# First pair of an attention and SwiGLU kernel: from both batches together to one batch after the other, with another fixed order of the parts

## The chip, the cores and the metric

The kernel runs on one core of one Trainium2 chip. The metric is the device time of one execution in microseconds (us); a time of the kernel is the median over several runs. The core has TensorE (PE in the profile; PEld is its weight load), VectorE (DVE), ScalarE (ACT), GpSimd (POOL) and SyncE (SP), which issues the DMAs. Work buffers are in SBUF; TensorE writes to PSUM, which is divided into banks.

## What is computed

Attention with 32 memories a head, for 8 batches, 8 heads, 576 positions and 64 values a head, and behind it a normalised SwiGLU block on 4608 tokens of 512 values:

```python
a = exp(phi - max(phi)); a = a / (sum(a) + 1e-09)
k_m = einsum('bhsm,bhsd->bhmd', a, k)
v_m = einsum('bhsm,bhsd->bhmd', a, v)
scores = (q @ k_m.T) / sqrt(64)
attn = softmax(scores)
x = (attn @ v_m), heads side by side
xn = x / sqrt(mean(x * x) + 1e-06) * rms_g
g = xn @ w_gate; val = xn @ w_val
out = (silu(g) * val) @ w_out
```

`w_gate` and `w_val` are 512 x 1536, `w_out` is 1536 x 512. All arrays are float32.

## The kernel before, in words

The eight batches are worked in four pairs, `pr` 0 to 3. The product `attn @ v_m` is never sent through the gate as `x`: `v_m` (with `rms_g` in it, `vm`) is multiplied with the weights first (`vw_steps`: `vp`, split into a high part `xh` and a low part `xl`), and the gate products `pg` and `pv` (`gv_steps`, L1069) then take the attention `at`, scaled by the token's root `rinv` and split into `ath` and `atl`, as their other operand. `x` itself is made once (`xp`, L845), for the sum of its squares alone. Behind the gate stand `sg` (silu, ScalarE), `hf` (product, VectorE), its parts `hh` and `hl`, and the output product `po` (L1126), summed in `acc` and stored. Products of high and low parts stand in for one float32 product.

Pair 0 has a path of its own, and it is what the change is about. For each batch `b` the k and v of a half (`load_half`, L331) and `phi` are loaded, `prep` makes the exponentials `e_bd`, and `kv_steps(b)` makes `kvp` (products of k or v with `e_bd`, L461, and with `ones`, L471), then on VectorE `si`, `im`, `kb` and `vb` (L480 to L496), on TensorE the transpose `kvt` (L511), and on ScalarE `km` (L519); `vt` becomes `vm` on GpSimd (L533). Then come the scores, by head pair `s` of four and by group of tiles (the 9 tiles of a batch are in `GROUPS` of 4 and of 5). One array holds both batches: `load_q` (L546) puts the q of batch `j` on every second partition, `q_steps` copies it in order (`qr`, L553), transposes it (`qtp`, L567) and copies it back (`qT`, L573). `score_steps` multiplies it with the `km` of both batches (`S`, L589), and VectorE makes the maximum `mxs` (L599), the difference `ex` (L603) and, behind the exponential of ScalarE (L608), the sum `sm` (L612 to L618). GpSimd divides, and the result stands in `first` (L624).

`x_steps(0)` then takes `first` by two tiles: transposes `tp` (L747), copies into `at` (L757), `xp` and its squares with their sums `ssq` (L856), the root chain `fin` in two groups of tiles (12 VectorE rows each, L866 to L891, result `rinv`), and for every tile a diagonal matrix of its `rinv` on ScalarE (`diag`, L803), with which TensorE multiplies `first`, so that transposing and scaling are one product (`ts`, L811). ScalarE copies the high part of `ts` out (`ath`, L830), VectorE subtracts it for the low part (`atl`, L826).

The pairs 1 to 3 go through `attend_steps` and the other branch of `x_steps`. Beside all this, the weights are loaded as `raw`, scaled by powers of two and split (`convert`: `wex`, L948 and L960 on VectorE, `wc` and `w` on GpSimd, L981).

What sets the order: every step above is appended to a list, `parts`, in the order of the program; `perform` then runs the parts in the order of the table `ISSUE`, and each engine's queue, SP's DMA queue too, takes its instructions in that order. No scheduler comes behind it. PSUM tiles of one bank are handed out by `bank`, from four buffers that rotate under one tag (L271); SBUF buffers are handed out by tags in the order in which the parts ask for them.

## Time and profile before

| | |
|---|---|
| median of three runs | 793.31 us (793.02 to 795.59) |
| the profiled execution | 792.07 us |
| its span, first to last instruction | 790.3 us |
| mean granted TensorE clock | 0.991 |
| PE busy | 748.9 us (95%) |
| PEld busy | 639.0 us (81%) |
| DVE busy | 471.8 us (60%) |
| ACT busy | 350.9 us (44%) |
| POOL busy | 244.4 us (31%) |
| DMA | 112.86 MB, 143 GB/s in the mean |

Busy times are of the profiled execution and are shares of its span. PE and PEld overlap. A row of the time line is one instruction or a few alike, with its start, its length, the engine, the line, the operation, what it writes and reads, and in brackets the idle time of the engine ahead of it and what ended that. A row of the waits says which engine waited for which, in how many pieces and for how long. In the stretches, the granted clock is a share of 2.4 GHz.

### The profile page before, as it was taken

How to read it: one execution, taken by the hardware profiler on the slowest of the kernel's cores; microseconds unless marked ns; L12 is line 12 of the kernel's file. 1: busy time of each engine (PE TensorE's matmuls, PEld its weight loads, DVE VectorE, ACT ScalarE, POOL GpSimd, SP SyncE). 2: the span in 40 equal slices, each digit the busy share in tenths (PEclk: the TensorE clock that was granted, in tenths of full speed). 3: DMA queues.
4: the chain of work that ended last, by engine and by line, in shares of the span. 5: the costliest groups of instructions: out<-in, count | busy, mean ns of one | idle time of the engine just before them, and what ended most of it. 6: DMA issues, size and time to landing. Idle time of an engine off the chain costs nothing.

```text
span 790.3 us, 18128 instructions
## 1 busy us (share of the span) xinstructions
PE 748.9 (95%) x7496; PEld 639.0 (81%) x7496; DVE 471.8 (60%) x956; ACT 350.9 (44%) x697; POOL 244.4 (31%) x209
## 2 busy tenths in 40 slices
PE   4777988999999999999999999899999999999998
PEld 2565766788887988888888888788888888888886
DVE  6698878888776676465565374655454422444443
ACT  1668767665555544532354334442432335232221
POOL 0244555354432223322433212221232212121212
PEclk9799999999999999999999999999999999999999
DMA  9947775856583652253153654222241334112113
GB/s 331 375 148 214 200 184 198 275 177 213 196 216 85 198 152 95 80 174 98 67 181 123 153 170 99 86 81 71 92 134 54 117 110 147 53 56 80 54 54 120
DMA packets 111722, 112.86 MB, mean 143 GB/s; under 512 B 61460, under 2 KB 77848, under 8 KB 111640
## 3 DMA queue, kind: packets, MB, share of 16 engines
q1 hardware_dynamic: 111640, 111.70, 45.2%
q8 instruction: 59, 0.97, 0.5%
q14 instruction: 23, 0.19, 0.1%
HBM read 89.66 MB, written 22.02 MB: 141 GB/s over the span
## 4 chain that ended last, share of the span: by engine, by line
PE 81%; DVE 6%; ACT 5%; DMA 4%; SPq 2%; issue 1%; POOL 0%; ACTq 0%; DVEq 0%
PE po L1126 36%; PE pg L1069 17%; PE pv L1069 17%; PE vp L1034 5%; PE xp L845 2%; SPq L645 2%; DMA kvs<-in_k_dram 1%; PE kvp L461 1%; DMA qs<-in_q_dram 1%; PE S L670 1%; ACT wex L944 1%; DVE phi L407 1%; ACT xh L1051 1%; DMA raw<-in_moe_w_out_dram 1%; ACT L1080 1%
## 5 line engine op out<-in xcount | busy, mean ns | idle before, releaser
L1100 POOL TENSOR_TENSOR hl<-hf,hh 128x512 fp32r<-128x512 f32 (+1 forms) x84 | 120.0, 1431 | 311.8 <-ACT hh L1095 297.9
L1085 DVE TENSOR_TENSOR hf<-pv,sg 128x256 f32<-128x256 f32 (+1 forms) x192 | 85.5, 452 | 153.1 <-PE pv L1069 110.1
L1126 PE MATMUL po<-oh,hh 128*128 128x512 f32 x432 | 172.2, 399 | 2.3 <-ACT acc L1135 1.4
L1080 ACT ACTIVATE sg<-pg 128x256 f32<-128x256 f32 (+1 forms) x192 | 77.6, 411 | 213.9 <-PE pg L1069 183.3
L1137 DVE TENSOR_TENSOR acc<-po,acc 128x512 f32<-128x512 f32 x180 | 121.0, 685 | 84.5 <-PE po L1126 84.0
L1126 PE MATMUL po<-oh,hl 128*128 128x512 f32 x432 | 170.2, 394 | 0.0
L1126 PE MATMUL po<-ol,hh 128*128 128x512 f32 x432 | 169.2, 392 | 0.0
L1095 ACT CAST hh<-hf 128x512 fp32r<-128x512 f32 (+1 forms) x96 | 64.5, 675 | 86.5 <-DVE hf L1085 86.2
L1126 PEld LDWEIGHTS po<-oh,hh 128*128 128x128 f32 x432 | 81.1, 188 | 21.8 <-ACT acc L1135 2.2
L1126 PEld LDWEIGHTS po<-oh,hl 128*128 128x128 f32 x432 | 81.2, 188 | 17.9
L1126 PEld LDWEIGHTS po<-ol,hh 128*128 128x128 f32 x432 | 81.2, 188 | 13.5
L1069 PE MATMUL pv<-ath,xh 128*128 128x320 f32 (+1 forms) x384 | 84.6, 301 | 4.3 <-ACT sg L1080 3.3
L1069 PE MATMUL pg<-ath,xh 128*128 128x256 f32 (+1 forms) x384 | 85.8, 305 | 2.4 <-DVE hf L1085 1.4
L1069 PE MATMUL pv<-ath,xl 128*128 128x320 f32 (+1 forms) x384 | 81.4, 293 | 0.0
L1069 PE MATMUL pg<-ath,xl 128*128 128x256 f32 (+1 forms) x384 | 81.3, 293 | 0.0
L1069 PE MATMUL pg<-atl,xh 128*128 128x256 f32 (+1 forms) x384 | 81.3, 293 | 0.0
L1069 PE MATMUL pv<-atl,xh 128*128 128x320 f32 (+1 forms) x384 | 81.3, 293 | 0.0
L1049 DVE TENSOR_TENSOR xl<-vp,xh 128x512 fp32r<-128x512 f32 x96 | 64.3, 682 | 28.0 <-ACT xh L1051 27.8
L1069 PEld LDWEIGHTS pg<-ath,xh 128*128 128x128 f32 x384 | 62.7, 188 | 16.7 <-issue 5.0
L1069 PEld LDWEIGHTS pv<-ath,xh 128*128 128x128 f32 x384 | 63.4, 188 | 15.3 <-ACT sg L1080 5.3
L1051 ACT CAST xh<-vp 128x512 fp32r<-128x512 f32 x96 | 54.3, 590 | 29.8 <-PE pv L1069 11.7
L1069 PEld LDWEIGHTS pv<-atl,xh 128*128 128x128 f32 x384 | 61.3, 188 | 0.0
(121 smaller groups left out, 998.0 us busy)
## 6 DMA issues: line engine op xcount, KB each, us to landing
wc<-wd SPq DMA_DIRECT2D x36, 512.0 KB, 5.5
oh<-od SPq DMA_DIRECT2D x36, 256.0 KB, 3.6
ol<-od SPq DMA_DIRECT2D x36, 256.0 KB, 3.9
out_dram<-acc SPq DMA_DIRECT2D x36, 256.0 KB, 2.2
q<-in_q_dram SPq DMA_DIRECT2D x96, 72.0 KB, 2.9
raw<-in_moe_w_val_dram SPq DMA_DIRECT2D x12, 512.0 KB, 4.7
raw<-in_moe_w_gate_dram SPq DMA_DIRECT2D x12, 512.0 KB, 4.5
raw<-in_moe_w_out_dram SPq DMA_DIRECT2D x12, 512.0 KB, 4.7
```

Source lines behind the costliest of these rows:

```text
L645: load(d["q", cc][32 * g:32 * g + 32, s], q[b, 4 * cc + 2 * s + h].rearrange("(r x) d -> r x d", r=32)[:, :, 32 * half:32 * half + 32],)
L845: nc.tensor.matmul(xp[64 * j:64 * j + 64, s, t - t0, P * cc:P * cc + P], st["at", pr][rows, t, cc, 64 * j:64 * j + 64], st["kb", 2 * pr + ...
L1034: nc.tensor.matmul(vp[32 * g:32 * g + 32, flip(b, cc), cc, :], vm[pr][rows, b, hp, 32 * (g % 2):32 * (g % 2) + 32], w[rows, hp, :], start= ...
L1049: V.tensor_tensor(out=xl[:, k], in0=src, in1=xh[:, k].bitcast(F32), op=ALU.subtract)
L1051: nc.scalar.copy(xs[i][0][:, k], src)
L1069: nc.tensor.matmul(pt[:, :N], l[:, flip(b, cc), cc, half * P:half * P + P], r[:, b, cc, t0:t0 + n, :].rearrange("p t x -> p (t x)"), start ...
L1080: nc.scalar.activation(sg[:, :N], acts[gi, b, 0][:, :N], AF.Silu)
L1085: V.tensor_tensor(out=acts[gi][:, :, b, :], in0=acts[gi, b, 1][:, :N].rearrange("p (t x) -> p t x", x=64), in1=acts[gi, b, 2][:, :N].rearr ...
L1095: nc.scalar.copy(hh, acts[gi].rearrange("p t b x -> p t (b x)"))
L1100: (V if gi and i < 12 else nc.gpsimd).tensor_tensor(out=hl, in0=acts[gi].rearrange("p t b x -> p t (b x)"), in1=hsplit[i, gi][0].bitcast(F ...
L1126: nc.tensor.matmul(po, l[:, tt, :], r, start=(m == 0), stop=(m == 5))
L1137: V.tensor_tensor(out=accs[key], in0=pt[0], in1=accs[key], op=ALU.add)
```

## The change

Pair 0 is worked batch by batch. `load_q(j, s, half)` loads the q of one batch and two heads onto 64 partitions, so that one tile of scores holds four heads of one batch; each batch has two `s` in place of the four for both. In the list, `q_steps`, `score_steps` and the new `first_steps` of batch 0 stand before batch 1's. `first_steps(j)` takes the place of the pair 0 branch of `x_steps`. It transposes `first` (`tp`) by pieces of 4, 4 and 1 tiles, copies them (the middle piece on VectorE), and packs two tiles into one `xp` of 128 partitions, so that five squares a batch are left. As a token's sum then stands on either half of the partitions, a small product with a constant `twice` (which GpSimd makes at the start) puts them in order (`ss`, two products a batch). One root chain a batch follows, 12 VectorE rows of 9 columns. `scaled` then multiplies `first` by the root on GpSimd (three pieces a batch), TensorE transposes the result (`ts`), and `put` makes the high and low parts, three and three a batch.

Also: `bank` takes the bank of each tile from a table `BANKS`, one digit a call, from four tags of one buffer each; 17 SBUF tags get their place by small tiles ahead of everything else; and the table `ISSUE` is new in full.

The diff, cut:

```diff
-ON_SCALAR = 21
+
+BANKS = (
+    "012301230123012312132031203120310231032103213203012101231231200232332320312310230302031203103213"
...
+)
 
 ISSUE = [
-    31, 0, 37, 12, 38, 39, 13, 1, 40, 19, 14, 15, 20, 42, 2, 3, 21, 16, 17, 4, 5, 34, 22, 23, 24, 36, 18, 6,
...
+    24, 2, 25, 26, 27, 28, 17, 18, 29, 50, 30, 19, 20, 21, 22, 8, 36, 23, 31, 1, 32, 33, 37, 38, 0, 39, 40,
...
+    tiny = persist.tile([P, 64], F32, name="tiny")
...
+    BANK = "".join(BANKS)
+    turn = [0]
+
     def bank(name, shape=None):
-        return ps.tile(shape or [P, 512], F32, tag="b", name=name, bufs=4)
+        turn[0] += 1
+        return ps.tile(shape or [P, 512], F32, tag="b" + BANK[turn[0] - 1], name=name, bufs=1)
...
+    for tag, n in (
+        ("acc0", 1), ("acc1", 1), ("hf0", 1), ("mc", 4), ("mxp", 2), ("sg", 2), ("xh", 2), ("si", 2), ("im", 2),
+        ("hh0", 3), ("hl1", 3), ("hl0", 3), ("hh1", 3), ("xl", 2), ("mxs", 2), ("sm", 2), ("hf1", 1),
+    ):
+        sb.tile([P, 1], F32, tag=tag, name=f"{tag}_first", bufs=n)
...
-    def load_q(s, j):
-        load(st["q", s][j::2], q[j, 2 * s:2 * s + 2].rearrange("h (p c) d -> p h (c d)", c=NT))
+    def load_q(j, s, half):
+        hp = 2 * half + s
+        load(
+            st["q", j][64 * half:64 * half + 64, s],
+            q[j, 2 * hp:2 * hp + 2].rearrange("h (p c) d -> p h (c d)", c=NT),
+        )
+
+    def twice():
+        st["twice"] = tw = sb.tile([P, 2, 2, 64], F32, tag="hl0", name="twice", bufs=3)
+        nc.gpsimd.memset(tw, 0.0)
...
+    def first_steps(j):
...
+        def both():
+            d["ss"] = tp = bank(f"ss{j}")
+            for i in range(2):
+                nc.tensor.matmul(
+                    tp[:, i:10 - i:2], st["twice"][:, i].rearrange("p a x -> p (a x)"), st["ssq"][:, j, :5 - i],
+                    start=True, stop=True,
+                )
...
+        def scaled(t0, n):
+            def f():
+                nc.gpsimd.tensor_tensor(
+                    out=st["first"][:, 1, j, t0:t0 + n], in0=st["first"][:, 0, j, t0:t0 + n],
+                    in1=r[:, t0:t0 + n].unsqueeze(2).broadcast_to([P, n, P]), op=ALU.mult,
+                )
+            return f
...
+        steps = []
+        for t0, n in PIECES:
+            steps += [turn(t0, n, 0), copy(t0, n)]
+        for u0 in range(0, 5, 2):
+            steps += [mm(u0)] + [square(x) for x in range(u0, min(u0 + 2, 5))]
+        steps += [both, root]
+        for t0, n in PIECES:
+            steps += [scaled(t0, n), turn(t0, n, 1), put(t0, n, 0), put(t0, n, 1)]
+        return steps
...
-            def diag(t):
-                def f():
-                    d["dg", t] = dg = st["first"][:, NT * 256 + t * P:NT * 256 + (t + 1) * P]
-                    nc.scalar.activation(dg, ident, AF.Copy, scale=rinv[pr][:, t:t + 1])
-                return f
...
-        if pr == 0:
-            return steps + [scaled(t0) for t0 in range(0, NT, 2)]
...
-    load_phi(1)
-    for cc in range(2):
-        for i in range(2):
-            load_half(0, cc, i)
-    add(prep(0, 0, 2), prep(0, 2, 4)[:-1], prep(1))
-    add(load_rg, put_rg)
-    first_q = [[lambda s=s, j=j: load_q(s, j) for j in range(2)] for s in range(HP)]
-    add(first_q[:2])
+    add([lambda cc=cc, i=i: load_half(0, cc, i) for cc in range(2) for i in range(2)])
+    add([lambda s=s, half=half: load_q(0, s, half) for s in range(2) for half in range(2)])
+    add(lambda: load_phi(1))
     add([lambda cc=cc, i=i: load_half(1, cc, i) for cc in range(2) for i in range(2)])
-    add(first_q[2:])
+    add([lambda s=s, half=half: load_q(1, s, half) for s in range(2) for half in range(2)])
+    add(prep(0, 2, 4)[:-1], prep(0, 0, 2), prep(1), load_rg, put_rg, twice)
     for b in range(2):
         add(*kv_steps(b))
-    for t0, n in GROUPS:
-        for s in range(HP):
-            add(q_steps(s, t0 == 0), score_steps(s, t0, n))
-    add(x_steps(0, lambda t: st["a"][:, t]))
+        for t0, n in GROUPS:
+            for s in range(2):
+                add(q_steps(b, s, t0 == 0), score_steps(b, s, t0, n))
+        add(first_steps(b))
```

How the order moves, at three places. First SyncE's queue of DMAs at the start of the program, behind the first `phi`; `kvs_134` and `kvs_152` hold the k and v of batch 0, `kvs_136` and `kvs_154` those of batch 1, `qs` the q, `raw` a weight. Before:

```order
L334 DMA kvs_134<-in_v_dram 128x2x576
L334 DMA kvs_136<-in_k_dram 128x2x576
L334 DMA kvs_136<-in_v_dram 128x2x576
L334 DMA kvs_136<-in_k_dram 128x2x576
L334 DMA kvs_136<-in_v_dram 128x2x576
L546 DMA qs_137<-in_q_dram 64x2x576
L546 DMA qs_135<-in_q_dram 64x2x576 x2
```

Now:

```order
L358 DMA kvs_152<-in_v_dram 128x2x576
L571 DMA qs_153<-in_q_dram 64x2x576 x4
L1001 DMA raw_345<-in_moe_w_gate_dram 128x4x256
L358 DMA kvs_154<-in_k_dram 128x2x576 x2
L358 DMA kvs_154<-in_v_dram 128x2x576 x2
L1001 DMA raw_461<-in_moe_w_val_dram 128x4x256
L571 DMA qs_155<-in_q_dram 64x2x576 x4
```

Four loads of q and one weight have moved ahead of the k and v of batch 1.

Second, TensorE's queue from the k and v products of batch 0 on (`kvp_194`; those of batch 1 are `kvp_298` before and `kvp_464` now). Before:

```order
L461 MATMUL kvp_194<-kvs_134,e_bd_126 32x128 x72
L471 MATMUL kvp_194<-ones,es_268 32x1 x8
L461 MATMUL kvp_298<-kvs_136,e_bd_127 32x128 x48
L511 MATMUL kvt_362<-ident,kb_356 128x128 x2
L461 MATMUL kvp_298<-kvs_136,e_bd_127 32x128 x24
L511 MATMUL kvt_362<-ident,vb_359 128x128 x2
L471 MATMUL kvp_298<-ones,es_295 32x1 x8
L567 MATMUL qtp_2_0_417<-ident,qr_2_0_365 128x128 x4
```

Now, a little behind the products of batch 0:

```order
L628 MATMUL S_1_0_365<-km_333,qT_1_0_349 64x64 x8
L605 MATMUL qtp_1_4_382<-ident,qr_1_4_376 128x128 x4
L535 MATMUL kvt_326<-ident,vb_329 128x128 x2
L605 MATMUL qtp_0_4_398<-ident,qr_0_4_379 128x128 x4
L605 MATMUL qtp_0_8_419<-ident,qr_0_4_379 128x128
L605 MATMUL qtp_1_8_421<-ident,qr_1_4_376 128x128
L628 MATMUL S_0_4_427<-km_333,qT_0_4_397 64x64 x10
L628 MATMUL S_1_4_446<-km_333,qT_1_4_381 64x64 x10
L485 MATMUL kvp_464<-kvs_154,e_bd_128 32x128 x72
L495 MATMUL kvp_464<-ones,es_425 32x1 x8
L683 MATMUL tp_0_572<-ident,first 128x128 x4
L605 MATMUL qtp_1_0_580<-ident,qr_1_0_569 128x128 x4
```

The k and v products of batch 1 now stand behind all the score products of batch 0, with the first transposes of `first` right behind them.

Third, GpSimd's queue, where the rows of `first` with `rinv` (L741) are the new `scaled`. Before:

```order
L624 TENSOR_TENSOR first<-ex_2_4_805,sm_2_4_896 128x5x64
L624 TENSOR_TENSOR first<-ex_3_4_835,sm_3_4_907 128x5x64
L981 TENSOR_TENSOR wc_947<-mi_1_831,wex_1_708 128x4x128
L981 TENSOR_TENSOR wc_947<-mi_1_869,wex_1_647 128x4x128
L981 TENSOR_TENSOR w_0_1068<-mi_0_1019,wex_0_984 128x512
```

Now:

```order
L660 TENSOR_TENSOR first<-ex_0_0_673,sm_0_0_707 128x4x64
L741 TENSOR_TENSOR first<-first,rinv_101 128x512
L660 TENSOR_TENSOR first<-ex_1_0_739,sm_1_0_789 128x4x64
L450 TENSOR_TENSOR es_815<-e_bd_127 128x256
L1052 TENSOR_TENSOR wc_818<-mi_1_810,wex_1_779 128x4x128
L660 TENSOR_TENSOR first<-ex_0_4_813,sm_0_4_828 128x5x64
L741 TENSOR_TENSOR first<-first,rinv_101 128x512
```

The scaling of batch 0 stands between the divisions of batch 1. From some 310 us of the trace of before to the end, TensorE's order is the same but for a few rows, and its last 97 rows are the same.

## Rows read from the trace of the kernel before

**Rows 1.** Stretches: busy us of PE, PEld, DVE, ACT, POOL, clock, DMA share, GB/s

```profile
10.00:20.00 10.00, 6.63 (x204) 5.22 (x207) 6.99 (x22) 2.51 (x3) 0.00 (x0) 1.00 1.05 392
20.00:30.00 10.00, 6.46 (x148) 4.28 (x132) 3.02 (x17) 3.97 (x8) 0.09 (x1) 0.60 1.07 378
30.00:80.00 50.00, 37.86 (x804) 30.50 (x810) 46.18 (x130) 39.87 (x92) 24.04 (x30) 0.94 0.69 216
80.00:140.00 60.00, 53.37 (x504) 41.87 (x487) 50.18 (x86) 43.42 (x85) 30.18 (x23) 1.00 0.73 200
140.00:200.00 60.00, 59.09 (x653) 49.73 (x652) 50.50 (x103) 34.81 (x69) 28.34 (x26) 1.00 0.68 225
310.00:790.30 480.30, 474.22 (x4154) 412.64 (x4152) 232.82 (x438) 168.03 (x343) 123.59 (x96) 1.00 0.32 101
```

**Rows 2.** Longest wait of TensorE after 200 us: us, times, longest

```profile
PE pv L1069 <- ACT sg L1080: 2.0, 1, 2.0
```

**Rows 3.** Longest wait of TensorE in the whole run

```profile
PE ts L811 <- ACT first L803: 5.4, 3, 2.7
```

**Rows 4.** Time line of VectorE, 27 to 33 us: start, us, instruction

```profile
27.96 0.16 DVE L480 TENSOR_SCALAR si<-kvp 128x1 f32<-128x1 f32 x1 [6.77 <-PE kvp L471]
...
30.13 0.72 DVE L960 TENSOR_SCALAR wex<-wex 128x512 int32<-128x512 int32 x1
...
32.74 0.91 DVE L599 TENSOR_REDUCE mxs<-S 128x8 f32<-128x256 f32 x2
```

**Rows 5.** Time lines of TensorE and, in the last row, ScalarE, 13 to 24 us

```profile
13.52 3.85 PE L461 MATMUL kvp<-kvs,e_bd 64*32 64x128 f32 x132 [0.46 <-DMA kvs<-in_v_dram]
...
19.53 0.89 PE L461 MATMUL kvp<-kvs,e_bd 64*32 64x128 f32 x44 [1.42 <-DMA kvs<-in_v_dram]
...
23.66 0.62 ACT L553 COPY qr<-qs 128x512 f32<-128x512 f32 x1 [8.71 <-DMA qs<-in_q_dram]
```

**Rows 6.** Groups by line and shape: count, busy us, mean ns, idle before

```profile
L573 ACT COPY qT<-qtp 128x512 f32<-128x512 f32 x8 | 4.7, 586 | 0.1
```

**Rows 7.** Stretch of 30 to 58 us, score rows alone: `mxs`, then `sm`; VectorE first

```profile
30.00:58.00 28.00, 6.70 (x16) 0.93 0.64 216
...
30.00:58.00 28.00, 6.31 (x24) 5.28 (x8) 0.93 0.64 216
```

**Rows 8.** Groups by line and shape: subtractions on VectorE out of PSUM

```profile
L1049 DVE TENSOR_TENSOR xl<-vp,xh 128x512 fp32r<-128x512 f32 x96 | 64.3, 682 | 28.0 <-ACT xh L1051 27.8
...
L826 DVE TENSOR_TENSOR atl<-ts,ath 128x256 fp32r<-128x256 f32 x8 | 3.3, 417 | 0.1
```

**Rows 9.** Products with the diagonal: two of the time line, then the group

```profile
56.34 2.08 PE L811 MATMUL ts<-first 128*128 128x128 f32 x8 [2.68 <-ACT first L803]
...
61.96 1.16 PE L811 MATMUL ts<-first 128*128 128x128 f32 x8 [0.65 <-ACT first L803]
...
L811 PE MATMUL ts<-first 128*128 128x128 f32 x36 | 6.0, 320 | 5.4 <-ACT first L803 5.4
```

**Rows 10.** Groups by line and shape: long pieces of GpSimd

```profile
L1100 POOL TENSOR_TENSOR hl<-hf,hh 128x512 fp32r<-128x512 f32 x48 | 63.3, 1319 | 183.2 <-ACT hh L1095 183.1
```

**Rows 11.** Time lines of VectorE and GpSimd, 44 to 49 us; groups, 20 to 140 us

```profile
44.07 0.42 DVE L948 TENSOR_SCALAR wex<-wex 128x512 f32<-128x512 f32 x1
...
47.92 0.90 DVE L948 TENSOR_SCALAR wex<-wex 128x512 f32<-128x512 f32 x1
...
47.13 1.41 POOL L624 TENSOR_TENSOR first<-ex,sm 128x320 f32<-128x320 f32 x2 [0.42 <-DVE sm L615]
...
L960 DVE TENSOR_SCALAR wex<-wex 128x512 int32<-128x512 int32 x19 | 9.3, 493 | 0.3
L948 DVE TENSOR_SCALAR wex<-wex 128x512 f32<-128x512 f32 x19 | 8.8, 463 | 2.6 <-ACT wex L944 2.4
```

**Rows 12.** Time line of VectorE, 56 to 83 us

```profile
56.54 0.22 DVE L618 RECIPROCAL sm<-sm 128x10 f32<-128x10 f32 x1
...
82.69 0.29 DVE L826 TENSOR_TENSOR atl<-ts,ath 128x128 fp32r<-128x128 f32 x1 [0.33 <-ACT ath L830]
```

More of the change, by code (lines that the diff above doesn't have):

```diff
@@ L541, in kv_steps, with q_steps @@
         )
-    def load_q(s, j):
-        load(st["q", s][j::2], q[j, 2 * s:2 * s + 2].rearrange("h (p c) d -> p h (c d)", c=NT))
-    def q_steps(s, first):
+    def load_q(j, s, half):
[8 more added lines that the diff above has]
+        for i in range(2):
+            rows = slice(64 * i, 64 * i + 64)
+            for a in range(2):
+                nc.gpsimd.tensor_copy(tw[rows, i, a], ident[rows, rows])
+        st["ssq"] = persist.tile([P, 2, 5], F32, tag="ssq0", name="ssq0")
+        nc.gpsimd.memset(st["ssq"], 0.0)
+    def q_steps(j, s, first):
         g0, gn = GROUPS[0 if first else 1]
         def order():
-            st["qr", s, g0] = qr = small(0, [P, gn, 2, 64], "qr", f"qr0_{s}_{g0}")
+            st["qr", j, s, g0] = qr = small(0, [P, gn, 2, 64], "qr", f"qr{j}_{s}_{g0}")
             nc.scalar.copy(
                 qr.rearrange("p c h d -> p h c d"),
-                st["q", s].rearrange("p h (c d) -> p h c d", c=NT)[:, :, g0:g0 + gn],
+                st["q", j][:, s].rearrange("p h (c d) -> p h c d", c=NT)[:, :, g0:g0 + gn],
             )
@@ L610, in total @@
         def total():
-            d["sm"] = small(0, [P, 2 * n, 1], "sm", f"sm0_{s}_{t0}")
+            d["sm"] = small(0, [P, 2 * n, 1], "sm", f"sm{j}_{s}_{t0}")
             V.tensor_reduce(out=d["sm"], in_=d["ex"], axis=AX.X, op=ALU.add)
@@ L620, in norm @@
         def norm():
-            if (s, t0) == (0, 0):
-                st["first"] = sb.tile([P, 4608], F32, tag="acc0", name="first")
-                st["a"] = st["first"][:, :NT * 256].rearrange("p (t m) -> p t m", m=256)
+            if "first" not in st:
+                st["first"] = sb.tile([P, 2, 2, NT, P], F32, tag="acc0", name="first")
             nc.gpsimd.tensor_tensor(
-                out=st["a"][:, t0:t0 + n, 64 * s:64 * s + 64].rearrange("p t (h m) -> p t h m", m=M),
+                out=st["first"][:, 0, j, t0:t0 + n, 64 * s:64 * s + 64].rearrange("p t (h m) -> p t h m", m=M),
                 in0=d["ex"].rearrange("p (t h) m -> p t h m", h=2),
@@ L727, in attend_steps, with x_steps @@
         )
-    def x_steps(pr, a=None):
-        tps, xps, srcs, d = {}, {}, {}, {}
+    def x_steps(pr):
+        tps, xps = {}, {}
         i = pr % 2
-        def turn(t0):
-            n = min(2, NT - t0)
-            def f():
-                if t0 == 0:
-                    st["at", pr] = persist.tile([P, NT, 2, P], F32, tag="at", name=f"at{pr}")
-                tps[t0] = tp = bank(f"tp{pr}_{t0}")
-                for t in range(t0, t0 + n):
-                    srcs[t] = src = a(t)
-                    for cc in (1, 0):
-                        o = 2 * (t - t0) + cc
-                        nc.tensor.transpose(
-                            out=tp[:, o * P:(o + 1) * P], in_=src[:, cc * P:(cc + 1) * P],
-                            identity=ident,
-                        )
-            return f
-        def copy(t0):
-            n = min(2, NT - t0)
-            def f():
-                (nc.scalar.copy if ON_SCALAR & (1 << t0 // 2) else V.tensor_copy)(
-                    st["at", pr][:, t0:t0 + n].rearrange("p t c x -> p (t c x)"), tps[t0][:, :256 * n]
-                )
-            return f
         def spread(t0, n):
@@ L894, in newton @@
                 return [g0, g1, g2]
-            steps = [f0, f1, f2] + [newton(a) for a in range(3)]
-            return chain(steps) if pr == 0 else steps
+            return [f0, f1, f2] + [newton(a) for a in range(3)]
         steps = []
         for t in range(NT):
-            if not pr and t % 2 == 0:
-                steps += [turn(t), copy(t)]
             if t % 2 == 0:
```

136 lines of the change are left out of this document (90 added, 46 removed), and 301 rows, old and new, of the table ISSUE.

## The prediction

> **What bounds the kernel now.** I read the stretches first. From 310 us to the end TensorE is busy 474.2 of 480.3 us, and its waits of the profile's kind after 200 us are a single one of 2.0 us and crumbs, so nothing is to be had there; from 140 to 200 us it is busy 59.1 of 60 [rows 1, 2]. What can move is the front: in 30 to 80 us TensorE is busy 37.9 of 50, in 80 to 140 us 53.4 of 60, which leaves 12.1 and 6.6 us of idling, and most of the first 30 us, which wait for data. In 30 to 80 us VectorE is busy 46.2 of 50 us and TensorE's clock is at its lower level, 1.2 GHz, for a part of the time (granted 0.94 in the mean, and 0.60 in 20 to 30 us). So VectorE sets the front from 30 to 80 us; behind 80 us VectorE (50.2 of 60) and TensorE (53.4 of 60) wait in turn.
>
> Then the waits of TensorE: the longest in the front is `ts` waiting for `first`, the nine diagonals that ScalarE makes out of `rinv`, 5.4 us in three pieces [rows 3]. Then VectorE's own row of time: it sits idle 6.77 us ahead of batch 1's first `si` at 27.96 us, and its first score row is at 32.74 us [rows 4]. That hole is what a batch-by-batch order can fill.
>
> The sum is made against the profiled execution, 792.07 us (span 790.3 and 1.8 us around it); the median of the runs, 793.31 us, is 1.24 us more, and I carry the differences over to that median. A measurement of this kernel can tell about 0.3%, 2.4 us, from no change.
>
> **The change part by part.**
>
> *Loads.* All bytes stay. Four loads of q for batch 0 and one of a 512 KB weight now stand ahead of batch 1's k and v. At the 392 GB/s of 10 to 20 us [rows 1] a 288 KB load takes 0.75 us and a 512 KB one 1.3 us, so batch 1's last v lands 4 x 0.75 + 1.3 = 4.3 us later. Before, its products still waited for a landing until 19.53 us [rows 5]; now the data are there at some 23.8 us. Batch 0's q follows the k and v of batch 0, whose products start at 13.52 us, by 3.0 us, some 16.5 us, where ScalarE now waits 8.7 us to copy the first q at 23.66 us [rows 5].
>
> *The hole on VectorE.* Batch 0's k and v products end as before at some 17.5 us (132 of 144 took 3.85 us, from 13.52 on [rows 5]), and its `kb` and `km` follow at some 21 us (1.9 us for `si` to `vb` as batch 1 takes now, then a transpose and a copy: an estimate). Then ScalarE has 13 rows between `km` and the last `qT` of this batch: copies of some 0.6 us [rows 5, 6] and a few shorter ones, 7 us, so the last score products run at some 29.5 us. Batch 1's 144 k and v products stand behind them in TensorE's queue and take 4.2 us: its `si` comes at 33.5 us, 5.5 us later than now. What has VectorE done by then? Its score rows are 6.70 + 6.31 = 13.0 us for the pair [rows 7], and of batch 0's half, 6.5 us, all but the last subtraction and the last sums and reciprocals stand ahead of batch 1's `si`: 4.7 us. Before, it had done 0.9 us of score rows by 33.5 us. It had also done batch 1's `si` to `vb` (from 27.96 to 30.13 us less a weight row of 0.4, and one `vb` more: 1.9 us) and a weight row more, that of 30.13 us with 0.7 us [rows 4]. So VectorE is ahead by 4.7 - 0.9 - 1.9 - 0.7 = 1.2 us. Bounds: 0, and the whole hole, 6.8 us; the low end is near, because batch 1 comes later by nearly as much as the hole is long.
>
> *Splitting into high and low.* Ten low parts on VectorE (eight of 417 ns, two short ones) become four of twice the size and two short ones; a 128x512 one out of PSUM takes 682 ns [rows 8]. 8 x 0.417 - 4 x 0.682 = 0.6 us saved. The 24 rows of the two root chains stay 24. VectorE's part is 1.2 + 0.6 = **1.8 us**, and it counts in full, since VectorE is full from 30 us on.
>
> *`ts`.* It was a product with a diagonal, 36 TensorE rows; it is now a transpose of an already scaled array, one row for a tile's column half, 18 in all, so 18 rows go. Eight of the 36 took 1.16 us at the full clock [rows 9]: 18 x 0.145 = **2.6 us** of TensorE. They lie in 56 to 81 us, where TensorE is not full; I count them in full because everything that TensorE does there pushes the same queue and it is full soon after. Bounds: 0 and, at the lower clock (eight took 2.08 us at 56 us), 4.7. The four new `ss` products add a step over TensorE to each root chain; by the nearest rows, those of `ts`, the four take 0.6 us at most. ScalarE is rid of nine diagonals, each at most the 0.62 us of its 128x512 copy [rows 5], so 5.6 us at most, and has one square more; the steps over TensorE and this I set off against each other, 0.
>
> *`scaled` on GpSimd.* Four pieces of 128x512 and two of 128x128: 1.32 us for a long one of two SBUF arrays [rows 10], and for the two short ones together 0.9 us, an estimate: 6.2 us in all. GpSimd is busy 24.0 of 50 us in this stretch [rows 1], which is the cover; without it a long piece stands bare between root and transpose. They replace the wait of `ts` for `first`, 5.4 us, by a wait for GpSimd of a like size. I take 0, between a gain of 5.4 and a loss of 6.2. `twice` and the small fills stand at GpSimd's start, where it is busy 0.1 us of the 20 from 10 us on [rows 1].
>
> *Exclusion.* VectorE's weight row at 47.92 us took 0.90 us where its twin at 44.07 us took 0.42; GpSimd had `first` running from 47.13 to 48.54 us [rows 11]. In 20 to 140 us the two scaling rows take 463 and 493 ns on average, 19 of each: 19 x 0.043 + 19 x 0.073 = 2.2 us above 0.42. The Trainium skill, "SBUF — State Buffer", section "Who interferes with whom", says that a VectorE row in a two-port mode, or with two SBUF inputs, and a GpSimd row lock each other out for a whole instruction. By that rule the new pieces could hold VectorE up for as long as they run, and the sum would lose 6.2 us. The trace agrees with a lockout in that row of 0.90 us, but the means say that few rows meet one. An order that avoids the meetings can save at most the 2.2 us; the new GpSimd rows add meetings, and if VectorE stood still for all of them that were 6.2 us. I take **0.8 us** saved, nearer to what the rows show, between +2.2 and -6.2.
>
> *Banks and tags* add no instruction. In the full stretch there is one wait of 2.0 us left [rows 2], which is the bound of what they can save there; I take 0. The order of TensorE from some 310 us to the end is nearly the same row by row, so the end cannot pay.
>
> Sum: 1.8 + 2.6 + 0.8 = 5.2 us, so 793.31 - 5.2 = **788.1 us** (a profiled execution near 786.9).
>
> **The rivals.**
>
> *More (782 us).* `scaled` of batch 0 is done while batch 1's scores run, so the wait for `first` vanishes instead of changing hands, and half of its 5.4 us shows; the exclusion goes altogether. 1.8 + 2.6 + 2.2 + 2.7 = 9.3, and with a hole filled better by 2 us, 11.3: 782. For it: TensorE's front idles 18.7 us in 30 to 140 us, so there is room. Against: VectorE has only 3.8 us left in 30 to 80 us.
>
> *Same, VectorE-bound (791.5 us).* Only VectorE's 1.8 us counts and TensorE's shorter queue becomes a longer wait for `hf`; 793.3 - 1.8 = 791.5. For it: VectorE's 46.2 of 50. Against: TensorE is the fuller engine behind 80 us.
>
> *Same, lockout (795 us).* As a mechanism of this kernel: the two-input root rows and weight rows of VectorE meet every one of the six new pieces and wait 6.2 us, with nothing saved elsewhere; 793.3 - 1.8 - 2.6 + 6.2 = 795.1. Against it: in 30 to 140 us GpSimd worked 24.0 + 30.2 us [rows 1], and VectorE's scaling rows were stretched by only 2.2 us. This case is the rule of the Trainium skill's page "SBUF — State Buffer" at full force.
>
> *Slower (797.5 us): batch 1 is late.* From the last reciprocal of the pair's scores at 56.54 us to the last low part of the pair at 82.69 us lie 26 us of serial work [rows 12]: copies, products, squares, root, scaling, transposes. If batch 1's half of that keeps its length and starts 5.5 us later with its `si`, every gate product of batch 1 and so the first 128x512 output products come 5.5 us later; one bare piece of `scaled` adds 1.3 us, the 2.6 us of `ts` come off: +4.2. It decides when batch 1's last `ath` lands later than some 85 us. For it: batch 1's data and products do come later. Against: half of the pair's work is then already out of the way, so its chain meets an emptier VectorE.
>
> **How the numbers follow.** The forecast (785 to 790.9) 0.45; more (below 785) 0.17; the two "same" cases 0.13 and 0.08; slower 0.17. Faster by over 0.3% (below 790.9): 0.62; within: 0.21; slower (above 795.7): 0.17. The range for 8 in 10 runs from 781.5 to 795.5: it takes in "more" with the bounds of exclusion, and both "same" cases, and leaves out most of "slower" and what lies below 781.5. Of the likeliest case alone: 785 to 790.9.
>
> **What would show it.** Right: the first score row of VectorE at 21 to 23 us instead of 32.7; batch 1's `si` at 32 to 35; no idle of VectorE over 3 us between 21 and 33 us; the last `ath` of the pair before 80 us; TensorE's idle of 30 to 140 us at some 14 us instead of 18.7, and its busy time of the program 2 to 3 us less; the stretches after 310 us alike. Wrong: TensorE waiting over 8 us for GpSimd ahead of `ts`, the scaling rows of VectorE at 0.55 us or more on average, or a new wait in the full stretch from 140 us on, which nothing here foresees. If TensorE idles more at the lower clock, because its short products of 18 to 30 us are spread thinner, the granted clock of 20 to 40 us shows that.

## The result: slower by 1.2%, and the profile after

| | before | after |
|---|---|---|
| median | 793.16 us (792.96 to 795.59, 4 runs) | 804.33 us (798.05 to 805.81, 4 runs) |
| the profiled execution, its span | 792.07, 790.3 us | 805.81, 804.0 us |
| mean granted clock | 0.991 | 0.984 |

The ratio is 1.0117 (interval 1.0077 to 1.0156): slower by some 9 us by the ratio and 11 by the medians, where 5.2 us less were forecast. The time lies above the range. Here and below a median is over all executions of a kernel, while a ratio leaves out those over 1.5% above the kernel's fastest, of which there were two: 806.6 us (second kernel of experiment 3) and 801.6 us (first of experiment 6).

Where it went is read from the stretches of after, with the columns of [rows 1]:

```profile
10.00:20.00 10.00, 5.70 (x163) 4.80 (x163) 4.78 (x10) 1.78 (x2) 0.00 (x0) 1.00 1.06 241
20.00:30.00 10.00, 6.69 (x95) 4.94 (x95) 8.01 (x28) 6.76 (x15) 1.94 (x3) 1.00 1.07 338
30.00:80.00 50.00, 37.57 (x844) 29.78 (x844) 39.34 (x115) 31.09 (x67) 25.53 (x30) 0.83 0.77 229
80.00:140.00 60.00, 48.88 (x417) 39.58 (x421) 48.46 (x81) 40.91 (x74) 26.83 (x22) 0.97 0.66 169
140.00:200.00 60.00, 59.36 (x711) 50.59 (x703) 53.01 (x111) 38.69 (x79) 31.38 (x27) 1.00 0.64 207
200.00:310.00 110.00, 105.81 (x1002) 91.56 (x1003) 72.17 (x131) 51.99 (x97) 36.96 (x31) 0.98 0.53 149
310.00:804.00 494.00, 486.43 (x4262) 421.14 (x4260) 244.90 (x456) 174.69 (x352) 127.18 (x99) 1.00 0.34 109
```

Of before, the stretch that [rows 1] leaves out:

```profile
200.00:310.00 110.00, 109.73 (x1067) 94.06 (x1066) 76.75 (x143) 56.98 (x102) 37.42 (x30) 1.00 0.55 160
```

The span is 13.7 us longer. TensorE's idle time from 10 to 140 us grew from 25.7 to 31.2 us (+5.5); from 200 to 310 us, a stretch that the prediction held for full, by 3.9; behind 310 us by 1.5; from 140 to 200 us it fell by 0.3. Its busy time grew by 3.1 us (748.9 to 752.0) though 18 rows of `ts` went and 8 of `ss` came, and the granted clock is lower in the mean (0.984, before 0.991): in 30 to 80 us it is 0.83, before 0.94, though in 20 to 30 us it is 1.00, before 0.60. That is the 13.7.

The waits of TensorE in after (us in all, times, longest); `sg` was 2.0 us, once, in [rows 2], and the 5.4 us of [rows 3] are gone. The longest in all, of `mt`, lies in the first 14 us but for 0.4; in the first 10 us TensorE was idle for 8.5 us before and after:

```profile
PE mt L401 <- DVE mc L394: 9.0, 4, 5.0
PE pv L1140 <- ACT sg L1151: 4.8, 2, 4.6
PE po L1197 <- ACT sg L1151: 3.5, 3, 2.7
PE kvp L485 <- DMA kvs<-in_v_dram: 3.4, 2, 1.8
```

The data come late. The core's DMA in 40 equal slices of 10 to 35 us: busy share in tenths, then GB/s. Before:

```profile
DMA  9999999999999999999999999999999999999999
GB/s 398 394 391 391 398 391 387 391 394 391 394 391 391 387 395 387 387 398 391 391 386 369 354 374 338 359 367 384 384 392 378 400 393 382 383 360 357 352 369 360
```

After:

```profile
DMA  9999999999999999999999999999999999999999
GB/s 413 402 406 291 140 147 170 199 232 269 234 234 212 172 186 144 206 349 390 391 384 387 394 398 380 396 374 377 352 239 173 216 225 207 187 218 242 212 218 201
```

The busy share shows nothing: the engines look full in both. The rate falls to some 200 GB/s twice, while the q of batch 0 and then of batch 1 is loaded; between, with k and v, it is at its old height. Batch 1's last v, which TensorE waits for, lands at 31.4 us (its products ran from 19.53 us on before [rows 5]):

```profile
31.41 4.19 PE L485 MATMUL kvp<-kvs,e_bd 64*32 64x128 f32 x144 [1.80 <-DMA kvs<-in_v_dram]
```

VectorE in after: the first score row, the new hole, batch 1's first `si` (27.96 us in [rows 4]) and the pair's last low part (82.69 us in [rows 12]).

```profile
23.24 0.42 DVE L636 TENSOR_REDUCE mxs<-S 128x8 f32<-128x256 f32 x1 [1.18 <-PE S L628]
...
35.36 0.43 DVE L1019 TENSOR_SCALAR wex<-wex 128x512 f32<-128x512 f32 x1 [3.16 <-ACT wex L1015]
35.75 0.16 DVE L504 TENSOR_SCALAR si<-kvp 128x1 f32<-128x1 f32 x1
...
88.87 0.68 DVE L755 TENSOR_TENSOR atl<-ts,ath 128x512 fp32r<-128x512 f32 x1
```

The second loss is on ScalarE. Its time line in after, at two places:

```profile
82.36 0.66 ACT L1015 ACTIVATE wex<-raw 128x512 f32<-128x512 f32 x1 [1.14 <-DMA raw<-in_moe_w_val_dram]
85.96 0.66 ACT L1015 ACTIVATE wex<-raw 128x512 f32<-128x512 f32 x1 [2.94 <-DMA raw<-in_moe_w_gate_dram]
86.52 1.22 ACT L1027 ACTIVATE mi<-raw 128x512 int32<-128x512 uint32 x2
87.64 0.42 ACT L1151 ACTIVATE sg<-pg 128x320 f32<-128x320 f32 x1
...
239.99 0.66 ACT L1015 ACTIVATE wex<-raw 128x512 f32<-128x512 f32 x1 [6.27 <-DMA raw<-in_moe_w_gate_dram]
240.55 0.75 ACT L1151 ACTIVATE sg<-pg 128x320 f32<-128x320 f32 x2
```

`sg` is ready to run, but stands in ScalarE's queue behind `wex` (the first step of a weight), and `wex` waits for a load. TensorE's next product waits for that `sg`:

```profile
88.12 0.54 PE L1140 MATMUL pv<-ath,xh 128*128 128x256 f32 x2 [4.61 <-ACT sg L1151]
...
241.03 0.50 PE L1197 MATMUL po<-oh,hh 128*128 128x512 f32 x1 [2.70 <-ACT sg L1151]
```

The load of `w_val` is late because SyncE's queue, which issues it, stands for 8.6 us before a load of q (L784) whose buffer TensorE's products `kvp` still read. First its wait, then its time line:

```profile
SPq L784 <- PE kvp L485: 8.6, 1, 8.6
...
65.23 0.33 SPq L998 DMA_DIRECT2D raw<-in_moe_w_out_dram  x1
73.92 2.67 SPq L784 DMA_DIRECT2D q<-in_q_dram  x4
76.69 0.56 SPq L1001 DMA_DIRECT2D raw<-in_moe_w_val_dram  x1
```

And each of the two waits costs more than its length. Stretches of after, columns as in [rows 1]: TensorE does nothing from 84 to 88 us and then runs 4 us at 0.57 granted, part of it at 1.2 GHz; likewise behind 241 us.

```profile
84.00:88.00 4.00, 0.00 (x0) 0.00 (x0) 1.35 (x4) 2.04 (x5) 0.00 (x0) 1.00 0.63 85
88.00:92.00 4.00, 3.79 (x15) 3.49 (x16) 2.37 (x5) 1.45 (x4) 2.57 (x3) 0.57 0.65 107
...
241.00:246.00 5.00, 4.97 (x17) 4.02 (x18) 2.55 (x5) 2.49 (x6) 0.00 (x0) 0.66 0.01 3
```

### The profile page after: what moved, and what is told of

It reads as the page before. It is cut to its first block, busy times and chain, and to the rows that moved or that the text cites. A ratio compares the mean times of both kernels' runs of the same rounds, so it can differ in the third digit from the quotient of the medians.

```text
span 804.0 us, 18086 instructions
## 1 busy us (share of the span) xinstructions
PE 752.0 (94%) x7486; PEld 643.0 (80%) x7486; DVE 476.3 (59%) x952; ACT 348.6 (43%) x687; POOL 251.7 (31%) x221
## 4 chain that ended last, share of the span: by engine, by line
PE 74%; DMA 10%; DVE 7%; SPq 4%; ACT 3%; issue 2%; POOL 0%; DVEq 0%; ACTq 0%; POOLq 0%
PE po L1197 33%; PE pg L1140 16%; PE pv L1140 16%; PE vp L1105 4%; SPq L784 3%; DMA q<-in_q_dram 2%; DMA kvs<-in_k_dram 2%; DMA qs<-in_q_dram 2%; PE xp L921 2%; PE kvp L485 1%; DMA raw<-in_moe_w_val_dram 1%; DVE qT L793 1%; DMA kvs<-in_v_dram 1%; DVE xl L1120 1%; DMA kv<-in_v_dram 1%
## 5 line engine op out<-in xcount | busy, mean ns | idle before, releaser
L1151 ACT ACTIVATE sg<-pg 128x256 f32<-128x256 f32 (+1 forms) x192 | 77.3, 411 | 202.6 <-PE pg L1140 168.1
L1197 PEld LDWEIGHTS po<-ol,hh 128*128 128x128 f32 x432 | 81.4, 189 | 13.8
L1140 PE MATMUL pv<-ath,xh 128*128 128x320 f32 (+1 forms) x384 | 85.7, 305 | 5.9 <-ACT sg L1151 4.8
L1140 PE MATMUL pg<-ath,xh 128*128 128x256 f32 (+1 forms) x384 | 85.1, 303 | 1.9 <-ACT sg L1151 1.0
L1140 PE MATMUL pv<-atl,xh 128*128 128x320 f32 (+1 forms) x384 | 81.8, 294 | 0.3 <-DVE atl L755 0.3
L1140 PE MATMUL pv<-ath,xl 128*128 128x320 f32 (+1 forms) x384 | 81.7, 294 | 0.0
L1140 PE MATMUL pg<-ath,xl 128*128 128x256 f32 (+1 forms) x384 | 81.6, 293 | 0.0
L1140 PE MATMUL pg<-atl,xh 128*128 128x256 f32 (+1 forms) x384 | 81.2, 293 | 0.0
L1140 PEld LDWEIGHTS pv<-ath,xh 128*128 128x128 f32 x384 | 64.0, 190 | 17.0 <-ACT sg L1151 5.5
L1140 PEld LDWEIGHTS pg<-ath,xh 128*128 128x128 f32 x384 | 63.2, 188 | 15.7 <-issue 5.7
L1140 PEld LDWEIGHTS pv<-atl,xh 128*128 128x128 f32 x384 | 61.8, 190 | 0.5 <-DVE atl L755 0.5
```

The costliest lines, as they stand in the source:

```text
L1140: nc.tensor.matmul(pt[:, :N], l[:, flip(b, cc), cc, half * P:half * P + P], r[:, b, cc, t0:t0 + n, :].rearrange("p t x -> p (t x)"), start ...
L1151: nc.scalar.activation(sg[:, :N], acts[gi, b, 0][:, :N], AF.Silu)
L1197: nc.tensor.matmul(po, l[:, tt, :], r, start=(m == 0), stop=(m == 5))
```

## The experiments

In the edits of the table `ISSUE` a number is a part: one load, one row of an engine or a few. The kernels from the third on carry the table on one line, so the line numbers shown of them are 154 lower than in after (L1140 is L986, L1151 is L997, L1015 is L861). Each is compared with the kernel before of the same session and chip, whose median was 793.4 to 794.9 us.

**1. Where a load of q puts its rows.** Before, the q of batch `j` went to every second partition; in the change it goes to 64 adjacent ones. The first kernel undoes this in the change, the second does it alone in the kernel before; the scores read the rows of `qT` accordingly.

```diff
-            st["q", j][64 * half:64 * half + 64, s],
+            st["q", j][half::2, s],
...
-        load(st["q", s][j::2], q[j, 2 * s:2 * s + 2].rearrange("h (p c) d -> p h (c d)", c=NT))
+        load(st["q", s][64 * j:64 * j + 64], q[j, 2 * s:2 * s + 2].rearrange("h (p c) d -> p h (c d)", c=NT))
```

> The change, with one thing different: the q of two heads lands on every second of the 128 partitions, as before the change, instead of on 64 adjacent ones, and the score products take every second column of the transposed q, so that the same numbers come out. In the trace of the change the loads of q for batch 0 and 1 follow each other by 1.2 us and more, the first four and the weight behind them take from 15.6 to 22.3 us, and the rate falls to 147 to 230 GB/s from 11 to 18 us. Theory A (a load to 64 adjacent partitions moves at half the rate and holds up everything behind it in the DMA queue): the loads of q land 0.75 us apart at 370 GB/s or more, the last v of batch 1 lands at 23 to 25 us instead of 31.4, and the kernel takes 787 to 794 us. Theory B (the new order itself puts batch 1 too late, whatever the rate): batch 1's data come sooner, but the kernel stays at 799 to 806 us.

> The kernel before, with one thing different: its q loads land on 64 adjacent partitions, as in the change, and the score products take their columns to match. Theory A: the seven loads of q that follow each other from 20 to 30 us land 1.2 to 1.8 us apart instead of 0.75, the first weight lands 3 to 7 us later, and the kernel takes 3 to 8 us longer than before, 796 to 801 us. Theory B: a load of q takes what it took, and the kernel stays within 2 us of 793.

Measured: the change with every second partition 797.92 us, ratio 1.0065 (1.0038 to 1.0091); the kernel before with adjacent partitions 799.56 us, ratio 1.0081 (1.0056 to 1.0105). The median's excess over before falls from 11.2 to 4.3 us in the one, which lies between the ranges of its two theories, and 6.0 us appear in the other, within the range of theory A. The rate in 10 to 35 us, first of the change with every second partition, then of before with adjacent ones:

```profile
GB/s 409 413 409 398 387 395 391 386 368 360 366 383 388 387 398 391 380 398 392 386 368 362 362 383 391 379 392 406 360 375 352 366 363 358 367 367 346 394 378 317
```

```profile
GB/s 413 413 402 402 383 398 391 387 398 394 383 394 395 221 195 199 151 214 199 206 218 229 214 218 210 210 212 193 215 188 188 177 240 282 331 340 220 213 218 187
```

So the same bytes by the same instruction go at some 380 GB/s or at some 205, by the partitions alone, and in both kernels that is worth 6 to 7 us by the medians (4 to 6 by the ratios; the intervals of the change, 1.0077 to 1.0156, and of the first kernel overlap at their ends). That the score products read other rows of `qT` is not what gains the time: their 144 rows took 6.2 us in after and 7.1 us in the first kernel. The Trainium skill, "SBUF — State Buffer", section "Door 1: The DMA port swizzle", says that partitions 0 to 63, or 64 to 127, reach only half of the 16 ports into SBUF, and gives 196 GB/s for partitions 0 to 63 against 328 for all 128, at 1 MiB a transfer; these runs agree on the half. Every second partition, which these runs show at the full rate, spreads over both halves.

**2. Order of the loads.** If batch 1 being late were the loss, its k and v should go ahead of batch 0's q: 11, 9, 12 and 10 ahead of 5, 4, 7 and 6 in the table of the change.

> The change, with one thing different: in SyncE's queue the four loads of batch 1's k and v stand ahead of the loads of q of batch 0, which still land on 64 adjacent partitions. Theory A: batch 1's last v lands at about 19.5 us, as before the change, and the slow q loads come behind it, so q of batch 0 lands from 21 to 27 us and batch 0's scores start some 6 us later; what is behind in the queue stays as late as in the change, and the kernel takes 797 to 805 us. Theory B (the place of batch 1's k and v in the queue is what counts): the kernel gets back most of the loss, 790 to 796 us.

Measured 810.0 us, ratio 1.0192 (1.0168 to 1.0217): slower than the change itself, and above both expectations. Batch 0 then has nothing to do, and TensorE waits 6.9 us for the first q:

```profile
24.54 1.11 PE L451 MATMUL qtp<-ident,qr 128*128 128x128 f32 x4 [6.86 <-ACT qr L437]
```

So it is not batch 1's place behind the q of batch 0 that costs the time: with this rate of loads the other order costs more.

**3. `sg` behind late weights.** On top of the first kernel of 1. The first edit takes the rows of two weights (823 to 828, 830 to 835) and 1006, the `wex` of a later one, behind the `sg` that they stood in front of (1137, 1437); the second takes the load of `w_val` (829) ahead of the load of q (441) on SyncE's queue.

> The change with q on every second partition (as in the first experiment, 797.9 us), and one thing more: at two places the scaling of a weight (wex, which waits for its load) is put behind the silu and the products that stood behind it: two weights at 75 to 82 us, one at 228 to 234 us. There TensorE waited 5.27 us (pv for sg at 77.5 us) and 2.76 us (po for sg at 232 us) while ScalarE stood idle in front of wex for 1.8, 2.95 and 6.3 us. Theory C (the new order puts silu behind a weight load that comes late, and TensorE waits for it): the two waits shrink to under 1 us each, and the kernel takes 790 to 794 us, 4 to 8 us less than the first experiment. Theory D (the weight itself is late, and what needs it is the next wait): the waits turn up at vp or po some microseconds later, and the time stays within 2 us of 798.

> The change with q on every second partition, and one thing more: in SyncE's queue one weight load (raw, w_val) that stood behind four loads of q of the next pair, issued at 71.2 us after SyncE had waited 8.2 us for the buffer of these q, now stands ahead of them. Theory C with its cause in the DMA queue: the load is issued at about 61 us, ScalarE's idle of 1.8 us in front of it goes, and since the second weight (w_gate) still comes at 80 us, TensorE's wait of 5.27 us at 77.5 us stays at 2 to 5 us; the kernel gains 0 to 2 us, 796 to 798 us. If the q loads get later by it than they can be, the kernel loses up to 2 us.

Measured 796.16 us, 1.0026 (1.0005 to 1.0048), and 796.91 us, 1.0023 (1.0005 to 1.0041). Each is a little under the kernel that it was built on (1.0065), with intervals that overlap at their ends; the first missed its 790 to 794 us, the second met its 796 to 798. In the first the two waits for `sg` went, but another came: in the new order the attention of the next pair stands behind the moved rows:

```profile
PE S L655 <- DVE qT L639: 8.0, 4, 4.6
```

In the second the first wait fell from 5.3 to 2.9 us; the load of the gate's weight is still late.

**4. Banks and tags.** Also on top of the first kernel of 1: the banks rotating as before, and the change without its 17 small tiles.

```diff
-        return ps.tile(shape or [P, 512], F32, tag="b" + BANK[turn[0] - 1], name=name, bufs=1)
+        return ps.tile(shape or [P, 512], F32, tag="b", name=name, bufs=4)
```

> The change with q on every second partition, but with the PSUM banks handed out from four rotating buffers again, instead of by the table. The prediction took the table for nothing. If that holds: within 2 us of 797.9 us, with TensorE's waits from 140 us on as they were. If the table saves waits in this order: 2 to 15 us slower, with new waits of TensorE for sg, hf or acc in the stretches from 140 us on.

> The change with q on every second partition, but without the 17 small tiles that give the SBUF tags their place ahead of everything else. The prediction took them for nothing: within 2 us of 797.9 us. If the places of buffers in SBUF matter for the time (which engines and loads meet): a difference of more than 2 us either way, with no wait that is new, but longer single instructions of VectorE or GpSimd.

Measured 802.93 us, 1.0114 (1.0077 to 1.0150), and 801.85 us, 1.0097 (1.0064 to 1.0130), against 1.0065 (1.0038 to 1.0091). The table of banks is probably worth a few us to the change; the intervals of the tags overlap too far to say. Neither can be the loss.

**5. More moves of the same kind.** The load ahead of q as in 3, and then: the `w_val` rows behind 1137, the gate's behind 294, 1006 behind 1437, and two parts of the gate (1160, 1149) ahead of four of the scores (451 to 454). Once with every second partition, once with adjacent ones.

> The change with q on every second partition, and the order mended where the fourth and fifth experiments showed a wait: the weight w_val is loaded ahead of the q of the next pair; the scaling of w_val stands behind the first silu and products, that of w_gate behind the copy of km; one scaling at 228 to 234 us stands behind two silus; and on TensorE two gate products stand ahead of the scores that wait for q. Theory C (what is left of the loss is waits in in-order queues behind late loads): of the 5.3 us at 77.5 us, or the 2.4 and 4.6 us that took their place in the fourth experiment, less than 4 us are left in 60 to 100 us, and the kernel takes 790 to 794 us, no slower than before. Theory D (another wait takes the place of each): waits of 6 us or more in 60 to 100 us, and the time stays at 795 to 798 us.

> The same mended order, but with q on 64 adjacent partitions, as the change has it: the other half of a table of two by two. If the slow loads and the queues cost independently: the kernel takes 6.4 us more than the one with the mended order and q on every second partition, which is what the first experiment gave back. If the queue waits come from the slow loads alone: it stays at 804 us.

Measured 801.09 us, 1.0102 (1.0064 to 1.0139), and 804.89 us, 1.0126 (1.0080 to 1.0172): a miss. TensorE now waits 8.8 us at 91.8 us for an `sg` (L997) that again stands behind a `wex`, which this time waits for GpSimd (`wc`):

```profile
88.59 0.66 ACT L861 ACTIVATE wex<-raw 128x512 f32<-128x512 f32 x1 [5.82 <-POOL wc L898]
...
91.31 0.42 ACT L997 ACTIVATE sg<-pg 128x320 f32<-128x320 f32 x1
```

The adjacent partitions cost 3.8 us by the medians here: less than the 6.4 of the one theory, at a time near the 804 us of the other. The intervals overlap, so neither is decided.

**6. Two moves only.** 829 ahead of 441, and 1006 behind 1437, on top of the first kernel of 1. The second kernel also takes two score parts of batch 0 (105, 106) and two transposes (114, 112) forward.

> The change with q on every second partition, with the weight w_val loaded ahead of the next pair's q (fifth experiment, 796.9 us) and with the one scaling at 228 to 234 us put behind the two silus that stood behind it (part of the fourth). The fourth and the eighth showed that this second move takes the stretch from 200 to 310 us back to no wait over 1 us, the eighth that moving more at 75 to 90 us makes a longer wait there. Theory C, held to these two places: no wait of TensorE over 1 us from 140 us on, one of about 3 us (pv for sg) at 60 to 100 us, and 792 to 795 us, that is, the change without its two faults takes what the kernel before takes. Theory D (the loss comes back elsewhere): 796 us or more.

> As the run beside it, and two steps of batch 0 earlier: its last subtraction and exponential, which stood behind batch 1's si and a weight on VectorE and held up ScalarE's copies of batch 1's q (idle of 1.35 us at 33.2 us, then a wait of TensorE of 1.8 us), stand ahead of them, and two groups of transposes of first stand ahead of the xp products on TensorE, where VectorE waited 1.6 us for them. If the front is still the bound: 1 to 3 us less than the run beside it, 789 to 793 us. If what is won in front of 60 us is waited away behind it, where the loads of the next pair come: within 1 us of it.

The first: 794.47 us against 794.04 (793.18 without the run of 801.6), ratio 1.0013 (0.9991 to 1.0036), 12 runs: no difference from before that can be told. From 200 to 310 us TensorE is full again (105.8 us busy in after, 107.1 in the first kernel of 1, 109.7 before):

```profile
200.00:310.00 110.00, 109.96 (x1026) 94.89 (x1025) 75.74 (x133) 55.11 (x99) 34.31 (x28) 1.00 0.50 143
```

Its profiled execution, the best of the twelve, took 788.72 us, what the prediction had said of the change. What the front is worth there: `xp` starts at 34.7 us (46.6 before), but the first gate product at 66.89 us, where before it stood at 66.51 and in after at 74.19. Here is that row of the first kernel of this step:

```profile
66.89 0.50 PE L986 MATMUL pv<-ath,xh 128*128 128x256 f32 x2
```

The 12 us that the first half wins are gone again at the gate; what takes them was not tested. The second kernel was to use them and missed: 798.77 us, 1.0063 (1.0042 to 1.0084), expected 789 to 793; its granted clock was 0.52 from 36 to 48 us.

**7. The load in another form.** On top of the first kernel of 6: each load brings two heads, one onto each half of the 128 partitions, with these two as the outermost dimension of the source.

```diff
-            st["q", j][half::2, s],
-            q[j, 2 * hp:2 * hp + 2].rearrange("h (p c) d -> p h (c d)", c=NT),
+            st["q", j][:, s, h],
+            q[j].rearrange("(a s h) (p c) d -> s h a p (c d)", a=2, s=2, c=NT)[s, h],
```

> The tenth experiment's kernel (794.5 us), with q in the layout of the change (four heads on two halves of 64 adjacent partitions), but each of the four loads of a batch brings one head of each half to all 128 partitions, in place of two heads to one half. Bytes, rows of 2304 bytes and the number of loads stay. Theory A, held to its reason (the number of adjacent partitions a load writes to sets its rate, not the layout of q): the loads land 0.75 us apart, batch 1's last v at 25 to 26 us, and the kernel takes 792 to 796 us, as the tenth. If it is the layout, not the load: 1.2 us and more apart, and 798 us or more. For the clock: where TensorE's granted clock stays full from 20 to 30 us in the profiled execution, that execution takes under 792 us, and where it falls there, over 793.

Measured 835.34 us, 1.0505 (1.0471 to 1.0539): a miss by far. The stretch of 18 to 24 us, DMA share and GB/s in the last two columns:

```profile
18.00:24.00 6.00, 0.00 (x0) 0.00 (x0) 1.74 (x11) 0.00 (x0) 0.00 (x0) 0.73 0.13 51
```

A share of 0.13 is 2 of 16 engines. The Trainium skill, "DMA: Bandwidth & Descriptors", section "Rules for kernel authors", says that the outermost dimension of a transfer sets how many engines take part, at most its size; with a size of 2 this run agrees. All 128 partitions on one side do not help when the other side's outermost dimension is 2.

**8. Why executions of one kernel differ.** The first kernel of 6 once more, unchanged, twice.

> The tenth experiment's kernel unchanged, profiled once more. Its twelve executions went from 788.7 to 801.6 us and its profiled one (788.7 us) kept TensorE's full clock from 18 to 36 us. If the spread is the granted clock in the front: this execution is slower where the clock from 18 to 50 us falls below 1.00 in the stretches (793 us or more then, under 791 otherwise), the loads land at the same times within 0.3 us, and the stretches behind 310 us take the same. If it is the loads: the rate in 12 to 36 us falls under 370 GB/s or the waits of TensorE for late loads from 60 to 100 us differ by more than 2 us at a like clock.

> The same kernel a third time, with the same expectation: time and granted clock from 18 to 50 us go together, loads and the waits of TensorE from 60 to 100 us stay within 1 us. If two executions differ by more than 3 us at the same clock in the front, something else sets the spread.

One execution each, on another chip than the twelve: 793.97 and 795.91 us. Three stretches of the best execution of 6, then of the first and of the second of these:

```profile
12.00:36.00 24.00, 17.73 (x465) 14.73 (x465) 18.41 (x59) 14.04 (x29) 3.88 (x6) 1.00 1.06 381
190.00:250.00 60.00, 59.24 (x610) 51.79 (x618) 39.30 (x79) 30.36 (x57) 21.35 (x20) 1.00 0.62 188
430.00:460.00 30.00, 29.78 (x345) 25.99 (x344) 16.71 (x38) 7.22 (x16) 6.26 (x7) 1.00 0.69 173
```

```profile
12.00:36.00 24.00, 18.41 (x430) 15.53 (x430) 17.25 (x59) 13.26 (x26) 2.92 (x5) 0.81 1.07 380
...
430.00:460.00 30.00, 28.06 (x322) 24.14 (x322) 12.99 (x29) 7.38 (x16) 7.12 (x7) 0.94 0.57 140
```

```profile
190.00:250.00 60.00, 56.67 (x581) 49.01 (x580) 37.64 (x79) 29.93 (x57) 19.53 (x18) 1.00 0.62 184
```

Same program, same loads; the first lost time at the lower clock in front and in a wait of 1.9 us near 437 us with a dip behind it, the second, among others, in waits of 1.5 and 1.2 us between 190 and 250 us. So part of the spread lies behind 310 us, against what was expected. Why such waits come in one execution and not in another stays open. It also means that one execution at 788.7 us is no gain: the median decides.

## Why the prediction was wrong

The changed kernel's time has three parts that the experiments take apart. **The loads:** 6.9 us of the excess of the median (11.2 to 4.3) go when the rows of q lie on every second partition, and 6.0 come when the kernel before gets the adjacent ones: shown in both directions, though the size is not sharp (3.8 us in the fifth experiment). **`sg` behind late weights:** two further moves take the excess from 4.3 to 0.4 us, with intervals that no longer overlap (1.0038 to 1.0091, 0.9991 to 1.0036), and the two waits went from 5.3 and 2.8 us to 3.7 and 0.5. More moves of the kind, in the fifth experiment, made a longer wait; so which order pays was found by trying. By the ratios the same steps read 1.17%, 0.65% and 0.13%, some 4 us each. **The gain of 5.2 us** does not show in any median: with both causes mended the new order ties with the old one, and the interval there (0.9991 at its low end) leaves room for a gain of 0.7 us at most. So the steps that counted VectorE's 1.8 us and TensorE's 2.6 us "in full" fail too: in that kernel `xp` starts 12 us earlier and the first gate product 0.4 us later than before.

By the prediction's steps:

- *Loads*, the step that failed. "At the 392 GB/s of 10 to 20 us [rows 1] a 288 KB load takes 0.75 us" took the rate of loads onto 128 or onto every second partition for a load onto 64 adjacent ones. It measured some 205 GB/s, so 1.4 us a load by that rate; batch 0's last v came later too (15.6 us, with full-rate loads 13.8), and batch 0's last q landed at 21.0 us, with full-rate loads at 16.8. Batch 1's last v was to land 4.3 us later, at some 23.8 us; it landed at 31.4, some 12 us later than the 19.5 of before. With full-rate loads it lands at 25.9, so 5.5 us of the miss are the rate, and the other 2.1 are there at either rate. Even so its products then start only at 29.15 us, because they stand behind batch 0's scores in TensorE's queue, as the step on the hole had it (29.5). The kernel's diff showed both forms of the address; nothing in the trace of before showed the slow one, and a loss was not bounded.
- *The order behind 80 us*, the second failure. The working followed the new order in the front only and left the rest at nothing, on the ground that TensorE's own queue behind 310 us is alike. TensorE's stop comes from ScalarE's queue (`wex` ahead of `sg`), and its cause from SyncE's (a weight behind q). The sign against it that the text named, "a new wait in the full stretch from 140 us on, which nothing here foresees", came at 241 us.
- *The hole on VectorE*, half right. First score row at 23.24 us (said 21 to 23; 21.24 with full-rate loads), batch 1's `si` at 35.75 us (said 32 to 35; 31.98 with full-rate loads). But VectorE idles 3.16 us ahead of 35.36 us, and it was busy 39.3 of 50 us from 30 to 80 us where it was to be the bound.
- *`ts`*, right in itself: 18 rows at 282 ns, by the group below, take as a group 3.1 us in place of 6.0 [rows 9], and the wait for `first` is gone. It did not show in the time: TensorE had 12.4 us of idling in 30 to 80 us. The new `ss` were put at four rows and 0.6 us at most; they are eight rows and took 1.5 us.

```profile
L683 PE MATMUL ts<-ident,first 128*128 128x128 f32 x18 | 3.1, 282 | 0.0
L755 DVE TENSOR_TENSOR atl<-ts,ath 128x512 fp32r<-128x512 f32 x4 | 2.7, 685 | 1.0 <-ACT ath L759 1.0
```

- *Splitting*, right: the four long low parts take 2.7 us and two short ones 0.6, so 3.3 for the former 3.9.
- *`scaled`*, right that it is covered: TensorE never waits for GpSimd ahead of `ts`, and the pieces take 5.1 us in all, where 6.2 were reckoned.
- *Exclusion*, about right: the scaling rows of VectorE from 20 to 140 us came to 436 ns (before 463) and 492 ns (493) on average, against 0.8 us foreseen and no sign of the lockout at full force [rows 11].

```profile
L1031 DVE TENSOR_SCALAR wex<-wex 128x512 int32<-128x512 int32 x16 | 7.8, 492 | 0.2
L1019 DVE TENSOR_SCALAR wex<-wex 128x512 f32<-128x512 f32 x17 | 7.4, 436 | 9.0 <-ACT wex L1015 9.0
```

- *Banks* were put at 0; the fourth experiment makes them more likely a few us in the change's favour.
- Of the signs named, idle time of TensorE from 30 to 140 us was to fall to 14 us and rose to 23.6; its busy time was to fall by 2 to 3 us and rose by 3.1; the last `ath` was to land before 80 us, and the low part made of it ran at 88.87.
- The rival *batch 1 is late* had the right side, and its point of decision (85 us) was passed. Its price, +4.2 us, was too small, since it knew neither the half rate of the loads nor the waits for `sg`.

## What to carry to other kernels

Where a change alters which partitions a load writes, price that load apart: the rate of the old form is no evidence for the new one, and the profile's DMA share does not show the difference, only GB/s does. When the order of a hand-written program moves, read every queue, those of ScalarE and SyncE above all: an instruction that waits for a load holds up what stands behind it, and TensorE pays for that far from the place that was changed. Time gained in front counts only if the next thing that the bound engine does comes earlier too.
